# Attention with top-1 experts on one core: side slots begun 39 tiles apart, and six weight tiles of the last one made on ScalarE and VectorE

## The chip, the cores and the metric

The kernel runs on one NeuronCore of a Trainium2 chip. The core has TensorE (PE in the profile; its weight loads are PEld), VectorE (DVE), ScalarE (ACT), GpSimd (POOL) and SyncE (SP), which here only issues DMAs. Each engine runs its own instructions strictly in the order of the program. The metric is the time of one execution on the device, in microseconds, as the median of several runs.

## The reference

```python
def _attn_ref(q, k, v, tau):            # 8 batches, 8 heads, 576 rows, 64 wide
    scores = scale * np.matmul(q, k.transpose(0, 1, 3, 2))
    thresh = np.max(scores, axis=-1, keepdims=True) - tau
    scores = np.where(scores >= thresh, scores, -1000000000.0)
    scores = scores - np.max(scores, axis=-1, keepdims=True)
    attn = np.exp(scores)
    attn = attn / (np.sum(attn, axis=-1, keepdims=True) + 1e-09)
    return np.matmul(attn, v)

def _moe_ref(x, modality_id, w_gate, modality_bias, w1, w2):   # x: 4608 x 512, 8 experts
    logits = x @ w_gate + modality_bias[modality_id]
    e_idx = np.argmax(logits, axis=1)
    ...
    for e in range(E):
        mask = e_idx == e
        h = np.maximum(x[mask] @ w1[e], 0.0)          # 512 -> 1024
        out[mask] = gate_w[mask, None] * (h @ w2[e])  # 1024 -> 512
```

The attention output, with heads side by side, is the `x` of the second function.

## The kernel before

**Attention** is cut into 288 tiles of 128 query rows of one head: 9 tiles for a pair of heads (`NI`), 36 for a batch (`PB`). The main loop (line 1055) takes one tile a step: scores on TensorE (`qk_half`, tile `s`), maximum on VectorE (`nm`), exponential on ScalarE (`e`), the threshold on VectorE (`pr`), transposes of `pr` back on TensorE (`tr`), and once per pair the product with the values (`pv_half`, tile `o`, line 458). Two more steps finish what lags behind, so the loop ends at step 290.

**Routing.** When a batch's four pairs are done, `gate` and `route_a` choose the expert of each row. `route_b` counts the rows ahead of each with small matmuls on TensorE (line 458 too, `bk<-oh,ltri`), and VectorE turns the counts into a place in a table (`pos`, then `posi`). Five indirect DMAs of GpSimd (`scatter`, line 621) write row number and gate weight there. For the last batch `route_b` stands at step 300.

**Slots.** The experts' work goes in slots: one expert and up to 512 of its rows. `slot` makes three lists: events (loads of the row table `tb` and of the weights, gathers of the rows, splits of the weights), transposes of the gathered rows (`xt`, line 765), and 64 TensorE pieces for a slot of 512 rows (48 for one of 256). A piece is three matmuls (line 809 for the first layer, 835 for the second), because each float32 operand is split in a high and a low part: `hi` is a rounded copy (lines 792 or 794), `lo` the difference (796). The 1024 hidden columns are eight blocks, `f_` = 0 to 7, and the pieces come in four runs of 16: first layer of blocks 0 to 3, second layer with them, first layer of blocks 4 to 7, second layer with those. ScalarE and VectorE make `hh` and `hl` of a first-layer block (819, 820), and the second layer needs them.

**Side slots** (seven, `SIDE`) take rows of batches that are routed already, while attention goes on. `begins` says at which step each starts; its pieces are spread over the steps up to the next start (`draw`, with weights by the step's place in the pair). What is left of the queue when the loop is over follows at two pieces a step from step 290 (line 1095). **Rest slots** (`last_slot`) take all other rows. `pick_rest` chooses them after the last routing, their first transposes stand at step `F0`, and their tiles come from pools that take over the memory of attention. In them ScalarE makes every `hi`, and VectorE the `lo` of the first layer; in side slots GpSimd makes both.

**Order.** TensorE and GpSimd run in the order that these steps and events give; on ScalarE, VectorE and SyncE a scheduler decides it when the program is built. Weight tiles `raw` of side slots share four buffers, split first-layer weights three, second-layer ones five.

Of the kernel before, what the change touches and what calls it, by code (L numbers as in the profile page):

```python
# [29 lines left out]
def tile_attn_moe(  # L30
# [13 lines left out]

    C = {'prep': [0, 1, 2], 'tr0': 6, 'pv0': 7, 'tr1': 12, 'sums': 13, 'pv1': 13, 'x': 14, 'gate': [15, 16, 17, 18], 'route': 18, 'routeb': 21, 'E0': 28, 'L0': 4, 'pick': -14, 'vld': 6, 'qkld': -3, 'pre': 2.5, 'wl': 3.5, 'rows': -11, 'gat': [-9.5, -8.5, -5, -4], 'xt': [-6, -5, -2, -1], 'lc': 21, 't3': 84, 'neg': 1.0, 'draw': [2, 2, 2, 2, 1, 2, 2, 1, 2], 'last': 36, 'te': 8, 'f0': 9.5, 'sc': 1, 'warm': 24,
         'wS': [-6, -4.7, -3.4, 3, 12.5, 14, 15.5, 21.5, 4.2, 5.4, 6.6, 7.5, 22.7, 23.8, 24.9, 25.8],
# [670 lines left out]

    def slot(where, group, nrow, WT=W, wq=lambda: wp, nbuf=(4, 3, 5), lo_eng=None, xq=None):

# [65 lines left out]
        def wsplit(which, f_):  # L785
            def f():
                raw = box.pop(("raw", which, f_))
                nb = nbuf[which]
                hi = wq().tile([P, 512], F32R, name=f"w{which}h", tag=f"w{which}h", bufs=nb)
                lo = wq().tile([P, 512], F32R, name=f"w{which}l", tag=f"w{which}l", bufs=nb)  # L790
                if xq:
                    nc.scalar.copy(out=hi, in_=raw)  # L792
                else:
                    nc.gpsimd.tensor_copy(out=hi, in_=raw)
                eng = lo_eng(which, f_) if lo_eng is not None else nc.gpsimd
                eng.tensor_tensor(out=lo, in0=raw, in1=hi.bitcast(F32), op=ALU.subtract)  # L796
                box[("w", which, f_)] = (hi, lo)
            return f
# [105 lines left out]
    def at(t, f):  # L904
        events.setdefault(t, []).append(f)
# [30 lines left out]

    begins = [b * PB + C['E0'] + (C['L0'] if z == len(SIDE) - 1 else 0) for z, (_, b) in enumerate(SIDE)]
    draw = [0] * (NSTEP + 2)
# [28 lines left out]
    for n0, (w, nb) in zip(begins, SIDE):  # L967
# [4 lines left out]
        at(n0 + C['pick'], choose)  # L972
        ev, pe, xts = slot(lambda cells=cells: cells["c"], lambda: group_bank(), nb * S, w)
        at(n0 - 0.45, lambda pe=pe: work_q.extend(f for _, f in pe))
        for x, f in xts:
            put(n0 + x, f)
        times = [t for t, _ in pe]
        k0 = upto[n0]

# [159 lines left out]
```

## Time and profile before

| | |
|---|---|
| time, median of 3 runs (lowest, highest) | 1069.17 us (1068.07, 1069.84) |
| the profiled execution: its time, its span | 1063.94 us, 1062.2 us |
| PE, PEld busy | 1011.3 us (95%), 802.7 us (76%) |
| DVE, ACT, POOL busy | 715.9 (67%), 639.9 (60%), 541.2 us (51%) |
| granted TensorE clock, mean | 0.99 of full speed |

The span runs from the first to the last instruction; the profiled execution's own time is 1.7 us more. Busy time of TensorE counts matmuls that overlap, with modelled ends, so a full share does not say that it could do no more. Times inside the profile are counted from the start of the span.

### The profile page before, as it was taken

The page shows a single profiled execution, that of the slowest core. Times are in us where ns is not written, and L with a number is a line of the kernel's source. Part 1 is how long each engine was busy: PE and PEld are TensorE (multiplying, and loading weights), DVE is VectorE, ACT ScalarE, POOL GpSimd, SP SyncE. Part 2 cuts the span into 40 slices and gives each one's busy share as a digit, 9 for nine tenths or more (in the row PEclk, how much of TensorE's full clock was granted, in tenths as well). Part 3 has the DMA queues.
Part 4 walks back from the last instruction along what each step waited for, and adds up shares of the span by engine and source line. Part 5 has one row for each costly group of instructions (what it writes and reads, how often), then busy time and mean ns, then how long its engine had stood idle before and what let it go on. Part 6 is the DMA issues. An engine that isn't in the chain of part 4 may idle for free.

```text
span 1062.2 us, 20681 instructions
## 1 busy us (share of the span) xinstructions
PE 1011.3 (95%) x6652; PEld 802.7 (76%) x6652; DVE 715.9 (67%) x1773; ACT 639.9 (60%) x1474; POOL 541.2 (51%) x727
## 2 busy tenths in 40 slices
PE   7798889999999999999999999999999997999996
PEld 6576668778777787777777777788777775788885
DVE  6888888787777676876587667776677544242542
ACT  5678777676767666656666666666666522434351
POOL 2233356486738653655466643755363746443441
PEclk8999999999999999999999999999999998999999
DMA  5656677577757754566548554566555314744430
GB/s 121 147 138 148 150 179 192 144 157 202 189 138 166 189 145 130 141 192 155 146 108 221 142 144 127 149 178 155 134 122 148 122 41 131 225 133 146 146 113 25
DMA packets 212711, 156.07 MB, mean 147 GB/s; under 512 B 100846, under 2 KB 172526, under 8 KB 212592
## 3 DMA queue, kind: packets, MB, share of 16 engines
q1 hardware_dynamic: 205392, 135.72, 51.0%
q0 software_dynamic: 7200, 18.92, 5.5%
q8 instruction: 55, 0.90, 0.4%
q14 instruction: 64, 0.52, 0.2%
HBM read 84.25 MB, written 19.48 MB: 98 GB/s over the span
## 4 chain that ended last, share of the span: by engine, by line
PE 78%; DVE 9%; issue 4%; DMA 3%; POOL 2%; ACT 2%; SPq 1%; POOLq 0%; DVEq 0%; ACTq 0%
PE s L369 15%; PE bk L458 14%; PE bk L809 11%; PE bk L835 10%; PE bk L420 10%; PE pm L835 6%; PE pm L809 5%; DVE pr L404 3%; DVE nm L386 3%; PE bk L311 2%; PE bk L449 1%; PE bk L507 1%; PE bk L765 1%; DMA raw<-in_moe_w_dram 1%; PE bk L539 1%
## 5 line engine op out<-in xcount | busy, mean ns | idle before, releaser
L386 DVE TENSOR_REDUCE nm<-s 128x1 f32<-128x576 f32 x288 | 216.7, 753 | 110.5 <-PE s L369 108.7
L404 DVE SCALAR_TENSOR_TENSOR pr<-s,nm,e 128x576 f32<-128x576 f32 x288 | 231.7, 815 | 74.6 <-ACT e L392 69.1
L392 ACT ACTIVATE e<-s,nm 128x576 f32<-128x576 f32 x288 | 214.8, 746 | 95.2 <-DVE nm L386 87.1
L369 PE MATMUL s<-km,q 128*128 128x288 f32 x1024 | 199.8, 317 | 21.1 <-DVE pr L404 16.5
L431 ACT COPY ptm<-bk 128x512 f32<-128x512 f32 x256 | 149.1, 582 | 58.2 <-PE bk L420 57.6
L369 PEld LDWEIGHTS s<-km,q 128*128 128x128 f32 x1024 | 146.9, 190 | 41.8 <-DVE pr L404 25.6
L420 PE MATMUL bk<-ident,pr 128*128 128x128 f32 x1152 | 173.7, 273 | 0.3 <-ACT y L843 0.2
L420 PEld LDWEIGHTS bk<-ident,pr 128*128 128x128 f32 x1152 | 142.1, 141 | 24.0 <-DVE hl L820 0.7
L458 PE MATMUL bk<-ptm,v_m 128*64 128x320 f32 (+1 forms) x1024 | 141.4, 413 | 0.1
L796 POOL TENSOR_TENSOR w2l<-raw,w2h 128x512 fp32r<-128x512 f32 x88 | 113.5, 1297 | 33.1 <-ACT w2h L792 28.7
L284 POOL CAST nk<-str 128x64 fp32r<-128x64 f32 x31 | 7.4, 240 | 228.2 <-ACT str L298 228.2
L458 PEld LDWEIGHTS bk<-ptm,v_m 128*64 128x64 f32 x1024 | 66.5, 136 | 48.6 <-issue 7.6
L849 POOL DMA_INDIRECT out_dram<-y,tb x37 | 38.7, 1046 | 107.9 <-DVE y L847 90.4
L433 ACT COPY rp<-pr 128x64 f32<-128x64 f32 x256 | 59.0, 248 | 55.8 <-DVE pr L404 53.8
L809 PE MATMUL bk<-xh,w1h 128*128 128x512 f32 (+1 forms) x212 | 85.3, 402 | 2.0 <-ACT xh L274 1.8
L809 PE MATMUL bk<-xl,w1h 128*128 128x512 f32 (+1 forms) x212 | 76.6, 361 | 2.1 <-DVE xl L275 2.1
L809 PE MATMUL bk<-xh,w1l 128*128 128x512 f32 (+1 forms) x212 | 76.3, 360 | 0.0
L835 PE MATMUL bk<-w2h,hh 128*128 128x512 f32 x176 | 75.7, 430 | 0.0
L796 POOL TENSOR_TENSOR w1l<-raw,w1h 128x512 fp32r<-128x512 f32 x56 | 71.6, 1279 | 4.5
L796 DVE TENSOR_TENSOR w1l<-raw,w1h 128x512 fp32r<-128x512 f32 x32 | 28.1, 882 | 65.3 <-ACT w1h L792 62.8
L835 PE MATMUL bk<-w2h,hl 128*128 128x512 f32 x176 | 69.5, 395 | 0.0
L835 PE MATMUL bk<-w2l,hh 128*128 128x512 f32 x176 | 68.9, 392 | 0.0
(203 smaller groups left out, 1982.4 us busy)
## 6 DMA issues: line engine op xcount, KB each, us to landing
raw<-in_moe_w_dram SPq DMA_DIRECT2D x176, 256.0 KB, 3.4
q<-nq SPq DMA_DIRECT2D x124, 256.0 KB, 4.5
km<-nk SPq DMA_DIRECT2D x124, 144.0 KB, 2.5
v_m<-in_v_dram SPq DMA_DIRECT2D x32, 256.0 KB, 4.6
xs<-xr SPq DMA_DIRECT2D x32, 256.0 KB, 5.7
k_m<-in_k_dram SPq DMA_DIRECT2D x62, 128.0 KB, 2.7
q_m<-in_q_dram SPq DMA_DIRECT2D x62, 128.0 KB, 3.1
vr<-in_v_dram SPq DMA_DIRECT2D x64, 16.0 KB, 3.6
```

Source lines behind the costliest of these rows:

```text
L369: nc.tensor.matmul(out=sps[:, hf, 0:SH], lhsT=a, rhs=x, start=(z == 0), stop=(z == len(passes) - 1))
L386: in_line(nc.vector.tensor_reduce(out=nm[:, 0:1], in_=sv, axis=AX.XY, op=ALU.max, negate=True), two)
L392: nc.scalar.activation(out=e, in_=sv, func=AF.Exp, bias=nm[:, 0:1])
L404: in_line(nc.vector.scalar_tensor_tensor(out=pr.rearrange("p (a x) -> p a x", a=2), in0=s2[n % 2][:, :, 0:SH], scalar=nm[:, 1:2], in1=e, o ...
L420: nc.tensor.transpose(out=ps[:, kc * P:(kc + 1) * P], in_=pr[:, kc * P:(kc + 1) * P], identity=ident)
L431: nc.scalar.copy(out=ptm[:, s, :, (c % 2) * P:(c % 2 + 1) * P], in_=pv)
L433: nc.scalar.copy(out=rp[:, i, :], in_=pr[:, SA:S])
L458: nc.tensor.matmul(out=o, lhsT=lhsT, rhs=rhs, start=start, stop=stop, skip_group_check=True)
L796: eng.tensor_tensor(out=lo, in0=raw, in1=hi.bitcast(F32), op=ALU.subtract)
L809: nc.tensor.matmul(out=ps[:, 0:WT], lhsT=a[:, cs], rhs=x[:, c, :], start=(c == 0 and z == 0), stop=(c == KC - 1 and z == 2))
L835: nc.tensor.matmul(out=ps, lhsT=h[:, ts], rhs=w, start=(z == 0 and y == 0), stop=(z == F2 - 1 and y == 2))
L849: i = _inst(nc.gpsimd.indirect_dma_start(out=out, out_offset=bass.IndirectOffsetOnAxis(ap=tb[:, t, 0:1].bitcast(U32), axis=0), in_=y, in_o ...
```

## The change

The last six side slots took turns of 36 tiles, except that the last began 4 tiles later. Now each slot of 512 rows begins 39 tiles after the one before it. The seven starts were steps 64, 100, 136, 172, 208, 244 and 284, and are 64, 100, 136, 175, 214, 253 and 292. Of the 416 pieces, 363 stood inside the loop and 53 behind it; now it is 348 and 68, so the last side slot lies wholly behind the loop. `F0` moves from step 311 to step 316, while the last batch's routing stays at step 300: between its matmuls and the first transposes of the rest slots stand 32 pieces where there were 22. In the last side slot the weights of blocks 5, 6 and 7 of both layers get their high part from ScalarE and their low part from VectorE.

```diff
-    C = {'prep': [0, 1, 2], 'tr0': 6, 'pv0': 7, 'tr1': 12, 'sums': 13, 'pv1': 13, 'x': 14, 'gate': [15, 16, 17, 18], 'route': 18, 'routeb': 21, 'E0': 28, 'L0': 4, 'pick': -14, 'vld': 6, 'qkld': -3, 'pre': 2.5, 'wl': 3.5, 'rows': -11, 'gat': [-9.5, -8.5, -5, -4], 'xt': [-6, -5, -2, -1], 'lc': 21, 't3': 84, 'neg': 1.0, 'draw': [2, 2, 2, 2, 1, 2, 2, 1, 2], 'last': 36, 'te': 8, 'f0': 9.5, 'sc': 1, 'warm': 24,
+    C = {'prep': [0, 1, 2], 'tr0': 6, 'pv0': 7, 'tr1': 12, 'sums': 13, 'pv1': 13, 'x': 14, 'gate': [15, 16, 17, 18], 'route': 18, 'routeb': 21, 'E0': 28, 'lag': 3, 'late': ((1, 5), (1, 6), (1, 7), (2, 5), (2, 6), (2, 7)), 'pick': -14, 'vld': 6, 'qkld': -3, 'pre': 2.5, 'wl': 3.5, 'rows': -11, 'gat': [-9.5, -8.5, -5, -4], 'xt': [-6, -5, -2, -1], 'lc': 21, 't3': 84, 'neg': 1.0, 'draw': [2, 2, 2, 2, 1, 2, 2, 1, 2], 'last': 36, 'te': 8, 'f0': 14.5, 'sc': 1, 'warm': 24,
...
-    def slot(where, group, nrow, WT=W, wq=lambda: wp, nbuf=(4, 3, 5), lo_eng=None, xq=None):
+    def slot(where, group, nrow, WT=W, wq=lambda: wp, nbuf=(4, 3, 5), lo_eng=None, xq=None, late=()):
...
-                if xq:
+                if xq or (which, f_) in late:
                     nc.scalar.copy(out=hi, in_=raw)
                 else:
                     nc.gpsimd.tensor_copy(out=hi, in_=raw)
-                eng = lo_eng(which, f_) if lo_eng is not None else nc.gpsimd
+                eng = lo_eng(which, f_) if lo_eng is not None else nc.vector if (which, f_) in late else nc.gpsimd
                 eng.tensor_tensor(out=lo, in0=raw, in1=hi.bitcast(F32), op=ALU.subtract)
...
-    begins = [b * PB + C['E0'] + (C['L0'] if z == len(SIDE) - 1 else 0) for z, (_, b) in enumerate(SIDE)]
+    begins = [b * PB + C['E0'] + C['lag'] * max(0, z - 2) for z, (_, b) in enumerate(SIDE)]
...
-        ev, pe, xts = slot(lambda cells=cells: cells["c"], lambda: group_bank(), nb * S, w)
-        at(n0 - 0.45, lambda pe=pe: work_q.extend(f for _, f in pe))
+        ev, pe, xts = slot(lambda cells=cells: cells["c"], lambda: group_bank(), nb * S, w,
+                           late=C['late'] if n0 == begins[-1] else ())
+        at(min(n0 - 0.45, NSTEP + 1), lambda pe=pe: work_q.extend(f for _, f in pe))
...
-        k0 = upto[n0]
+        k0 = sum(FC * KC + FC * (x // P) for x, _ in SIDE[:begins.index(n0)])
```

The order of the instructions moves with it at three places that matter below. The first is VectorE just behind the routing matmuls of the last batch. Before, the ranks went straight on to the table places:

```order
L602 TENSOR_TENSOR pos_11486<-bk0_162,base_144 128x48
L604 COPY base_144<-pos_11486 128x8
L605 TENSOR_TENSOR pos_11486<-pos_11486,creg_119 128x40
L657 SCALAR_TENSOR_TENSOR left_11550<-done_145,base_144 1x8
L607 TENSOR_TENSOR pos_11486<-pos_11486,oh_11444 128x40
```

The same place of the changed kernel:

```order
L602 TENSOR_TENSOR pos_11409<-bk3_165,base_144 128x48
L796 TENSOR_TENSOR w1l_11639<-raw_11569,w1h_11638 128x512
L820 SCALAR_TENSOR_TENSOR hl_11399<-bk1_163,hh_11398 128x512
L604 COPY base_144<-pos_11409 128x8
L605 TENSOR_TENSOR pos_11409<-pos_11409,creg_119 128x40
L657 SCALAR_TENSOR_TENSOR left_11465<-done_145,base_144 1x8
L607 TENSOR_TENSOR pos_11409<-pos_11409,oh_11371 128x40
```

The low part of the last side slot's first-layer weights of block 6 and the `hl` of its block 3 now stand inside the chain. The second place is SyncE behind the table load of the first rest slot (`tb`). Before, that slot's own first-layer weights followed it:

```order
L739 DMA tb_11650<-tab_140 128x4x2
L775 ISA
L775 DMA raw_11727<-in_moe_w1_dram 128x4x128
L775 ISA
L775 DMA raw_11747<-in_moe_w1_dram 128x4x128
```

In the changed kernel:

```order
L739 DMA tb_11619<-tab_140 128x4x2
L779 ISA
L779 DMA raw_11633<-in_moe_w2_dram 128x512
L775 ISA
L775 DMA raw_11710<-in_moe_w1_dram 128x4x128
L775 ISA
L775 DMA raw_11729<-in_moe_w1_dram 128x4x128
```

`raw_11633` is the side slot's second-layer weight of block 7; it moved behind the table load. The third place is ScalarE in the same stretch. Before, the `hh` of blocks 4, 5 and 6 of the side slot (`hh_11618`, `hh_11673`, `hh_11702`) came first, and one cast of a rest slot's weight stood ahead of block 7's (`hh_11719`):

```order
L819 ACTIVATE hh_11618<-bk3_165 128x512
L819 ACTIVATE hh_11673<-pm_11626 128x512
L819 ACTIVATE hh_11702<-pm_11681 128x512
L792 CAST w1h_11777<-raw_11727 128x512
L819 ACTIVATE hh_11719<-pm_11706 128x512
L792 CAST w1h_11815<-raw_11747 128x512
```

In the changed kernel, where `w2h_11689` and `w1h_11671` are the side slot's block 7 and `hh_11652` and `hh_11685` its blocks 4 and 5:

```order
L792 CAST w2h_11689<-raw_11633 128x512
L792 CAST w1h_11755<-raw_11710 128x512
L792 CAST w1h_11793<-raw_11729 128x512
L792 CAST w1h_11671<-raw_11592 128x512
L819 ACTIVATE hh_11652<-pm_11629 128x512
L792 CAST w1h_11843<-raw_11767 128x512
L792 CAST w2h_11872<-raw_11782 128x512
L792 CAST w1h_11890<-raw_11819 128x512
L792 CAST w2h_11979<-raw_11835 128x512
L819 ACTIVATE hh_11685<-pm_11664 128x512
L792 CAST w2h_11989<-raw_11862 128x512
L792 CAST w2h_12004<-raw_11882 128x512
```

Every cast but `w1h_11671` takes a weight that SyncE loads behind the table. The `hh` of blocks 6 and 7 follow only behind the last of these rows.

## Rows read from the trace of the kernel before

**Rows 1.** Windows: us, busy us (instructions) of PE, PEld, DVE, ACT, POOL, clock, DMA share, GB/s

```profile
500.00:820.00 320.00, 318.39 (x2121) 250.74 (x2120) 230.93 (x602) 204.99 (x478) 170.69 (x227) 1.00 0.58 146
...
868.40:902.80 34.40, 28.07 (x113) 21.22 (x113) 19.06 (x59) 9.76 (x17) 24.05 (x23) 0.85 0.34 102
...
881.40:884.80 3.40, 3.23 (x8) 2.61 (x9) 0.00 (x0) 0.00 (x0) 0.12 (x1) 0.55 0.00 0
884.80:891.30 6.50, 4.19 (x17) 2.80 (x16) 2.05 (x4) 2.24 (x4) 3.29 (x4) 1.00 0.70 197
891.30:898.20 6.90, 5.78 (x19) 4.30 (x18) 2.48 (x4) 2.94 (x6) 5.26 (x4) 0.51 0.92 309
```

**Rows 2.** Chain that ended last, inside the loop: start us, us, what

```profile
601.32 2.84 PE bk L458 x20
...
629.04 2.84 PE bk L458 x20
...
659.19 2.84 PE bk L458 x20
...
717.04 2.84 PE bk L458 x20
...
721.74 0.70 PE bk L809 x3
...
743.40 2.84 PE bk L458 x20
...
772.93 2.84 PE bk L458 x20
```

**Rows 3.** Timeline of PE behind the loop: start, us, what [idle before <-releaser]

```profile
868.48 0.20 PE L458 MATMUL bk<-oh,ltri 128*128 128x48 bf16 x1
...
880.21 0.50 PE L809 MATMUL pm<-xh,w1h 128*128 128x512 f32 x1 [2.27 <-POOL w1h L794]
...
881.57 0.80 PE L809 MATMUL pm<-xh,w1l 128*128 128x512 f32 x1 [0.63 <-POOL w1l L796]
...
889.76 0.50 PE L835 MATMUL pm<-w2h,hh 128*128 128x512 f32 x1 [2.20 <-ACT hh L819]
...
893.23 1.09 PE L765 MATMUL bk<-ident,xg 128*128 128x128 f32 x4 [1.12 <-DMA xg<-xs,tb]
...
899.19 0.60 PE L765 MATMUL bk<-ident,xg 128*128 128x128 f32 x4
...
902.85 0.40 PE L809 MATMUL pm<-xh,w1h 128*128 128x512 f32 x1
...
919.60 0.50 PE L835 MATMUL pm<-w2h,hh 128*128 128x512 f32 x1 [1.40 <-ACT hh L819]
```

**Rows 4.** Timeline of DVE: the ranks, the table places, a low part of a weight

```profile
868.82 0.21 DVE L602 TENSOR_TENSOR pos<-bk,base 128x48 f32<-128x48 f32 x1 [1.38 <-PE bk L458]
...
873.00 0.15 DVE L612 CAST posi<-posf 128x5 int32<-128x5 f32 x1
...
895.37 0.69 DVE L796 TENSOR_TENSOR w1l<-raw,w1h 128x512 fp32r<-128x512 f32 x1 [2.97 <-ACT w1h L792]
```

**Rows 5.** Timeline of POOL: the last of the five table scatters

```profile
878.57 0.97 POOL L621 DMA_INDIRECT tab<-pay,posi  x1 [0.30 <-issue]
```

**Rows 6.** Timeline of SP: table load of the first rest slot, then weights

```profile
884.33 0.38 SPq L739 DMA_DIRECT2D tb<-tab  x1
885.38 1.87 SPq L775 DMA_DIRECT2D raw<-in_moe_w_dram  x3
```

**Rows 7.** Waits of SP from 860 to 900 us: in total, times, longest

```profile
SPq L739 <- DMA tab<-pay,posi: 3.0, 1, 3.0
```

**Rows 8.** Timeline of ACT: first and eighth cast of that slot's weights, an hh between

```profile
888.60 0.62 ACT L792 CAST w1h<-raw 128x512 fp32r<-128x512 f32 x1 [9.96 <-DMA raw<-in_moe_w_dram]
889.12 0.59 ACT L819 ACTIVATE hh<-pm 128x512 fp32r<-128x512 f32 x1
...
898.02 0.62 ACT L792 CAST w2h<-raw 128x512 fp32r<-128x512 f32 x1 [1.16 <-DMA raw<-in_moe_w_dram]
```

## Prediction

> **What bounds the kernel now.** I read the windows first. From 500 to 820 us TensorE is busy for 318.39 of 320.00 us at full clock, and every other engine for less than three quarters of that [rows 1]. The reader is to see that the loop is bound by TensorE, so a piece of side-slot work that leaves the loop takes its TensorE time with it. The last batch's routing matmuls start at 868.48 (R below), and the first piece of a rest slot at 902.85 [rows 3]; in the 34.40 us between, TensorE is busy for 28.07 at a mean clock of 0.85 [rows 1]. The timeline of TensorE shows why. It stops for 2.27 and 0.63 us for block 7's first-layer weight of the last side slot, which GpSimd makes behind the scatters; for 2.20 us for the `hh` that follows; for 1.12 us for gathered rows; and later, at 919.60, for 1.40 us for an `hh` of a rest slot [rows 3]. Sum: 7.6 us. In two stretches the clock is at its lower level of 1.2 GHz: 0.55 over 3.23 busy us and 0.51 over 5.78 [rows 1], which costs 3.23 x 0.45 + 5.78 x 0.49 = 4.3 us. Ahead of the first such stretch stands the stop of 2.27, ahead of the second the one of 2.20. So some 12 us behind R are open to be won or lost.
>
> **Term 1: fewer pieces ahead of R.** 15 pieces leave the loop. Their price is read from the chain, where the same matmuls of line 458 return once a pair: 27.72 us from 601.32 to 629.04 with 16 pieces between by the program's order, 26.36 from 717.04 to 743.40 with 14; 30.15 from 629.04 to 659.19 with 16, 29.53 from 743.40 to 772.93 with 15 [rows 2]. Three pieces fewer take 1.36 + 0.62 = 1.98 us off, 0.66 each. The three matmuls of a piece stand there with 0.70 [rows 2], the upper bound; a loop that in part waits for other engines would give less, and I bound it by 0.50, well below what the two comparisons give (0.68 and 0.62). I take 0.66: 15 x 0.66 = -9.9 us (-7.5 to -10.5).
>
> **Term 2: from R to the first piece of a rest slot.** This is a chain from VectorE to the weights. Before: `pos` starts at R + 0.34, `posi` ends at 873.15 = R + 4.67 [rows 4], the last scatter starts 5.42 later [rows 5], the table load is issued 5.76 behind that [rows 6], after a wait of 3.0 for the scatters [rows 7], and the first weight load 1.05 later [rows 6]. The eighth cast of those weights starts 12.64 behind that issue, the first 3.22 [rows 6, 8].
>
> Now the low part of block 6's weight (0.69 [rows 4]) and an `hl` (a like operation, taken as 0.69) stand ahead of the copy of `base` on VectorE. The low part needs ScalarE's cast (0.62 [rows 8]), and that cast needs the buffer that block 3's last first-layer matmul frees, about at R. The copy follows at R + 0.62 + 0.69 + 0.69 = R + 2.0 instead of R + 0.55: +1.5 us (1.2 to 1.6). So `posi` ends at R + 6.2, the last scatter starts at R + 11.6, the table is loaded at R + 17.4 and the first weight load goes at R + 18.4.
>
> That first load is now the side slot's second-layer weight of block 7, and eight of the rest slot follow. SyncE issues in order, so it can't go before the table. On ScalarE the `hh` of blocks 5, 6 and 7 stand among or behind the casts of these nine, so TensorE, once it has done what it can, waits for loads. Two waits follow.
>
> First, block 7's first layer. TensorE reaches it 28 pieces behind R at 0.70 each, R + 20.0. Its cast stands behind three casts of new loads, the first of which can start at R + 18.4 + 3.2 = R + 21.6; four casts and a low part later the weight is there, at R + 24.1 or a little after. A stop of 4.1 us takes the place of 2.27 + 0.63 + 2.20 = 5.1.
>
> Second, and later, so that it decides: the last load. Nine loads land 12.64 + 0.85 behind the first issue (the ninth, 256 KB, at the 309 GB/s of the busiest stretch [rows 1]), at R + 31.9. A cast (0.62), two `hh` (0.59 each [rows 8]) and the `hl` (0.69) end at R + 34.4. Then TensorE does the rest of a piece, two sets of transposes (0.60 each [rows 3]) and four pieces, 4.2 us: R + 38.6. TensorE stops on the way for longer than the 2.20 that preceded the second low-clock stretch, so I add one stretch of half clock like the first (3.23 x 0.45 = 1.4): R + 40.0. Against 34.4 that is +5.6 us (+4.2 without the clock; to +8 with the slower loads below).
>
> Here a page speaks for less. The first stretch of loads runs at 197 GB/s and a DMA share of 0.70, the second at 309 and 0.92 [rows 1]. The Trainium skill, "DMA: Bandwidth & Descriptors", section "Where 436 GB/s comes from", says that a transfer from HBM to SBUF is bound by the HBM side at some 358 GB/s; by that figure nine loads and four gathers of 262 KB, 3.4 MB, would take 9.5 us instead of 13.5, and the sum would be 4 us lower (an estimate). No stretch here reaches it.
>
> **Term 3: pieces that stand later.** The last side slot has 8 pieces left when the rest slots begin where it had 3 (56 of 64 done, before 61). Five at 0.70: +3.5 us. The other ten of the fifteen lie inside term 2, under its waits.
>
> **Term 4: the stop at 919.60.** The `hh` that TensorE waits for there stands behind casts whose loads came late [rows 3]; by the new order no cast of a late load stands ahead of it: -1.4 us (0 to -1.5).
>
> **Costs that are hidden.** Six casts (0.62) and six subtractions (0.69) go to ScalarE and VectorE; GpSimd's took 5.26 / 4 = 1.3 us each in the last stretch [rows 1]. In the loop VectorE and ScalarE are busy for 230.93 and 204.99 of 320 us, so there is room; behind R their places cost what term 2 says. In turns of 39 tiles, the split of block 7 in a normal side slot waits for a buffer for up to 0.9 tile (about 2.8 us) on GpSimd, with gathers behind it; GpSimd is busy for 170.69 of 320 us [rows 1], and the rows are gathered tiles ahead. If that cover failed, TensorE would stop for up to 2.8 us in each of four slots. The last slot's last gather, near the end of the loop, has the same cover less some 1 us. The rows that each pick takes are the same, so no slot changes its size.
>
> **Sum.** -9.9 + 5.6 + 3.5 - 1.4 = -2.2 us against the profiled execution's 1063.94, 1061.7 there. The median of the runs is 1069.17, 5.2 above that execution; taken off the median, the forecast is 1067.0.
>
> **Rivals.** *The loads are slower* (it ends slower than before). Gathers and nine loads, 13 x 262 KB = 3.4 MB, run throughout at the 197 GB/s of the stretch at 884.80 [rows 1]: they take 17.3 us instead of 13.5, +3.8, and TensorE stands long enough for a second half-clock stretch like the one at 891.30, of which some 1.7 us are not waited out anyway. Sum +3.3: 1072.5. It decides when the first rest piece lies past R + 42.2 (no gain) or R + 44.4 (slower by 2.1). For it speaks that the last `hh` are queued behind nine casts; against it that the first half of the old loads ran at that rate and the second at 309.
>
> *The loads come as they are issued* (a larger gain). The first three issues take 1.87 us [rows 6], 0.62 each, and the first lands after 3.2. If all nine keep that, the last is there at R + 18.4 + 8 x 0.62 + 3.2 = R + 26.6, the casts of ScalarE are hidden by block 7's pieces, and the first rest piece comes at about R + 35: sum -7.2, 1062.0. Against it stand the old loads, of which the eighth needed 12.64. The skill's 358 GB/s ("DMA: Bandwidth & Descriptors", same section) would lie near this case, at about -6.
>
> *The loop gives back less.* If waits on ScalarE and VectorE take the place of the pieces, 0.50 each, 15 give -7.5 and the sum is +0.2: 1069.4, no change. For it: side-slot pieces are the filler between the attention's steps. Against it: both comparisons of [rows 2].
>
> **How the numbers follow.** The forecast as worked out has 0.50, its own range is 1065.0 to 1069.2 (term 2 from 4.2 to 7.0, term 1 by 0.8 either way); the larger gain 0.18, the smaller loop gain 0.15, the slow loads 0.17. A measurement of this kernel can tell about 0.2%, 2.1 us, from no change; the runs before spread over 1.8. The forecast lies at that edge: of its 0.50 some 0.26 fall beyond it, 0.23 within, 0.01 slower. Larger gain: 0.17 faster, 0.01 same. Loop: 0.01 faster, 0.12 same, 0.02 slower. Slow loads: 0.01 same, 0.16 slower. Sums: faster 0.44, same 0.37, slower 0.19. The range from 1062.5 to 1071.0 cuts off the outer parts of the first and the last rival, about 0.1 on either side.
>
> **What would show it.** Term 1: the marks of line 458 come closer by 0.66 us for each piece fewer, R lies near 858.6. Term 2: `posi` ends at R + 6.2 with a low part and an `hl` ahead of the copy, the table is issued at R + 17.4, TensorE stops about 4 us ahead of block 7's first layer for a cast, then again for an `hh` behind casts that wait for loads, and the first rest piece stands near R + 40 with a stretch at about half clock before it. Term 4: no stop of over 1 us in the first rest slot for an `hh`. The prediction is wrong if R moves by less than 7.5 us, if the table is issued before R + 16, or if the last of the nine casts starts before R + 28 or past R + 36.

## The result, and the profile after

The changed kernel took 1054.70 us (median of 4 runs, 1053.85 to 1055.24) beside 1068.62 for the kernel before (1066.30 to 1069.84): ratio 0.9882, 95% interval 0.9865 to 0.9900. That is 13.9 us faster, below the range of 1062.5 to 1071.0. Its profiled execution took 1054.34 us, that of before 1063.94: 9.6 us between the two traces. The other 4.3 us are runs of before that took longer than its profiled one, and no trace shows them.

In the later sets of runs the gain was smaller. Three controls of the changed kernel (after_again, after_third, after_fourth), on the chips that the record numbers 12, 3 and 1 (for the first set it names none), gave 0.9962 (0.9948 to 0.9977), 0.9955 (0.9938 to 0.9973) and 0.9942 (0.9922 to 0.9962), 5 to 8 us. Each is a ratio to the kernel before in the same set. The experiments below are read against these controls.

The windows of the changed kernel (us, then busy us and instructions of PE, PEld, DVE, ACT and POOL, clock, DMA share, GB/s), which answer to [rows 1]:

```profile
500.00:820.00 320.00, 317.57 (x2124) 248.74 (x2123) 231.74 (x602) 207.36 (x483) 176.27 (x229) 1.00 0.61 149
856.60:891.80 35.20, 32.65 (x144) 25.37 (x143) 19.77 (x65) 15.13 (x26) 18.18 (x17) 0.95 0.42 121
...
879.60:883.10 3.50, 3.50 (x9) 2.74 (x10) 2.17 (x3) 1.99 (x5) 1.49 (x3) 0.51 1.04 385
```

The loop is as full as it was. Behind the routing matmuls TensorE is busy for 32.65 us where it was busy for 28.07, in nearly the same time. The timeline of TensorE there, which answers to [rows 3]:

```profile
856.67 0.20 PE L458 MATMUL bk<-oh,ltri 128*128 128x48 bf16 x1
...
878.76 0.50 PE L809 MATMUL pm<-xh,w1h 128*128 128x512 f32 x1 [2.14 <-ACT w1h L792]
...
886.32 0.50 PE L835 MATMUL pm<-w2h,hh 128*128 128x512 f32 x1 [0.34 <-ACT hh L819]
...
891.74 0.40 PE L809 MATMUL pm<-xh,w1h 128*128 128x512 f32 x1
```

R moved from 868.48 to 856.67, by 11.8 us. The first rest piece stands at R + 35.1, where it stood at R + 34.4. The stops between are 2.14 and 0.34 us in place of 2.27, 0.63, 2.20 and 1.12. The chain on VectorE, which answers to [rows 4]:

```profile
857.02 0.21 DVE L602 TENSOR_TENSOR pos<-bk,base 128x48 f32<-128x48 f32 x1 [0.24 <-PE bk L458]
857.33 0.69 DVE L796 TENSOR_TENSOR w1l<-raw,w1h 128x512 fp32r<-128x512 f32 x1
857.94 0.68 DVE L820 SCALAR_TENSOR_TENSOR hl<-bk,hh 128x512 fp32r<-128x512 f32 x1
858.54 0.16 DVE L604 COPY base<-pos 128x8 f32<-128x8 f32 x1
...
859.20 0.36 DVE L662 SCALAR_TENSOR_TENSOR th<-th_lo,left 1x72 f32<-1x72 f32 x2
...
859.50 0.15 DVE L612 CAST posi<-posf 128x5 int32<-128x5 f32 x1
```

The low part and the `hl` stand ahead of the copy as forecast, which comes at R + 1.87. But `posi` ends at R + 2.98, not R + 6.2. The same stretch of the kernel before, first VectorE, then GpSimd, shows what was missed:

```profile
870.59 2.48 DVE L662 SCALAR_TENSOR_TENSOR th<-th_lo,left 1x72 f32<-1x72 f32 x2
```

```profile
870.45 2.54 POOL L796 TENSOR_TENSOR w2l<-raw,w2h 128x512 fp32r<-128x512 f32 x2
```

Two small operations (`th`), 0.18 us each in the changed kernel, took 1.24 each while GpSimd subtracted, and ended with its second subtraction. In the changed kernel GpSimd splits nothing there. The rest of the chain (GpSimd's last scatter; SyncE; ScalarE's first and last cast of the nine loads and the two `hh` behind), which answers to [rows 5 to 8]:

```profile
865.08 0.97 POOL L621 DMA_INDIRECT tab<-pay,posi  x1 [0.30 <-issue]
```

```profile
871.62 0.37 SPq L739 DMA_DIRECT2D tb<-tab  x1
872.26 0.35 SPq L779 DMA_DIRECT2D raw<-in_moe_w_dram  x1
```

```profile
875.01 0.62 ACT L792 CAST w2h<-raw 128x512 fp32r<-128x512 f32 x1 [6.03 <-DMA raw<-in_moe_w_dram]
...
885.15 0.62 ACT L792 CAST w2h<-raw 128x512 fp32r<-128x512 f32 x1 [0.45 <-DMA raw<-in_moe_w_dram]
885.67 1.08 ACT L819 ACTIVATE hh<-pm 128x512 fp32r<-128x512 f32 x2
```

The table load goes at R + 14.95 (forecast 17.4), the first weight load at R + 15.6 (18.4), the last cast starts at R + 28.5 (31.9) and the last `hh` ends at R + 30.1 (33.7).

### The profile page after: what moved, and what is told of

Read it like the earlier page. It is cut to its first block, busy times and chain, and to the rows that moved or that the text cites. A ratio compares the mean times of both kernels' runs of the same rounds, so it can differ in the third digit from the quotient of the medians.

```text
span 1052.4 us, 20681 instructions
## 1 busy us (share of the span) xinstructions
PE 1008.2 (96%) x6652; PEld 802.1 (76%) x6652; DVE 715.2 (68%) x1779; ACT 643.5 (61%) x1480; POOL 531.0 (50%) x715
## 5 line engine op out<-in xcount | busy, mean ns | idle before, releaser
L369 PE MATMUL s<-km,q 128*128 128x288 f32 x1024 | 199.5, 317 | 20.5 <-DVE pr L404 15.4
L796 POOL TENSOR_TENSOR w2l<-raw,w2h 128x512 fp32r<-128x512 f32 x85 | 111.2, 1315 | 31.2 <-ACT w2h L792 27.0
L809 PE MATMUL bk<-xh,w1h 128*128 128x512 f32 (+1 forms) x208 | 82.8, 398 | 0.9 <-ACT xh L274 0.9
L835 PE MATMUL bk<-w2h,hh 128*128 128x512 f32 x164 | 70.9, 432 | 0.0
L796 POOL TENSOR_TENSOR w1l<-raw,w1h 128x512 fp32r<-128x512 f32 x53 | 68.0, 1283 | 4.3
L796 DVE TENSOR_TENSOR w1l<-raw,w1h 128x512 fp32r<-128x512 f32 x35 | 31.1, 891 | 52.2 <-ACT w1h L792 52.1
L835 PE MATMUL bk<-w2h,hl 128*128 128x512 f32 x164 | 64.6, 394 | 0.0
L835 PE MATMUL bk<-w2l,hh 128*128 128x512 f32 x164 | 64.3, 392 | 0.0
```

The costliest lines, as they stand in the source:

```text
L369: nc.tensor.matmul(out=sps[:, hf, 0:SH], lhsT=a, rhs=x, start=(z == 0), stop=(z == len(passes) - 1))
L809: nc.tensor.matmul(out=ps[:, 0:WT], lhsT=a[:, cs], rhs=x[:, c, :], start=(c == 0 and z == 0), stop=(c == KC - 1 and z == 2))
L835: nc.tensor.matmul(out=ps, lhsT=h[:, ts], rhs=w, start=(z == 0 and y == 0), stop=(z == F2 - 1 and y == 2))
```

## The experiments

"Span behind R" is the span less R, taken from the first line of `ltri` in each trace. Each ratio is that to the kernel before in the same set of runs.

| run | median us (before beside it) | ratio, 95% interval | R | first rest piece | span behind R |
|---|---|---|---|---|---|
| before, two traces | | | 868.5; 877.6 | R + 34.4; 35.1 | 193.7; 194.2 |
| changed, first | 1054.70 (1068.62) | 0.9882, 0.9865 to 0.9900 | 856.7 | R + 35.1 | 195.7 |
| after_again | 1067.86 (1073.10) | 0.9962, 0.9948 to 0.9977 | 871.8 | R + 34.6 | 195.1 |
| after_third | 1068.12 (1072.98) | 0.9955, 0.9938 to 0.9973 | 870.3 | R + 34.7 | 194.9 |
| after_fourth | 1067.13 (1075.44) | 0.9942, 0.9922 to 0.9962 | 870.0 | R + 35.2 | 195.7 |
| lag_only | 1073.98 (1074.04) | 1.0008, 0.9989 to 1.0026 | 870.4 | R + 41.1 | 201.4 |
| late_only | 1073.20 (1074.04) | 0.9991, 0.9970 to 1.0012 | 878.5 | R + 33.0 | 195.3 |
| late_f0 | 1072.14 (1073.10) | 0.9994, 0.9979 to 1.0008 | 876.4 | R + 36.0 | 194.1 |
| last_only | 1073.11 (1074.04) | 0.9996, 0.9979 to 1.0013 | 876.5 | R + 36.3 | 196.4 |
| lag2 | 1081.76 (1072.98) | 1.0087, 1.0056 to 1.0118 | 887.0 | R + 34.1 | 192.2 |
| pool_busy | 1068.75 (1074.04) | 0.9956, 0.9937 to 0.9975 | 870.1 | R + 36.1 | 196.4 |
| sc3 | 1068.71 (1075.44) | 0.9944, 0.9927 to 0.9961 | 869.0 | R + 35.2 | 195.4 |
| f0_12 | 1069.54 (1072.98) | 0.9962, 0.9940 to 0.9984 | 870.1 | R + 32.6 | 196.3 |
| w17_first | 1071.35 (1073.10) | 0.9983, 0.9962 to 1.0005 | 870.5 | R + 38.1 | 198.7 |
| act_manual | 1067.20 (1072.98) | 0.9941, 0.9922 to 0.9961 | 870.4 | R + 35.0 | 195.6 |
| act_f0_17 | 1064.04 (1075.44) | 0.9911, 0.9885 to 0.9938 | 869.3 | R + 33.7 | 193.3 |
| act_f0_17b | 1067.82 (1076.00) | 0.9938, 0.9919 to 0.9958 | 870.8 | R + 35.0 | 193.4 |
| act_f0_19 | 1068.82 (1075.44) | 0.9955, 0.9934 to 0.9977 | 870.6 | R + 35.6 | 196.0 |
| dve_lo | 1070.26 (1076.00) | 0.9946, 0.9928 to 0.9965 | 873.1 | R + 34.2 | 192.9 |

### The parts of the change, one by one

The starts alone:

```diff
-'late': ((1, 5), (1, 6), (1, 7), (2, 5), (2, 6), (2, 7))
+'late': ()
```

> The changed kernel with the six late weight tiles back on GpSimd; the starts stay 39 tiles apart. Theory 1: part of the gain comes from the chain behind the routing matmuls (at R), because GpSimd no longer splits weights there, which held the scatters and stretched VectorE's small operations (0.63 and 1.24 us each before, 0.18 after). Then posi ends at R + 4.5 or later instead of R + 2.98, the table load goes 1.5 us or more later than R + 14.95, and the time is 1056.5 to 1060. Theory 2: the pieces that leave the loop carry the whole gain. Then the time stays within 2 us of 1054.7.

The gain is gone, but not by the chain: `posi` ended at R + 3.4. The timeline of TensorE:

```profile
896.54 0.80 PE L809 MATMUL pm<-xh,w1h 128*128 128x512 f32 x1 [6.12 <-POOL w1h L794]
...
905.69 0.51 PE L835 MATMUL pm<-w2h,hl 128*128 128x512 f32 x1 [1.55 <-DVE hl L820]
```

GpSimd splits the weight of block 7 behind the rest slot's gathers, and TensorE waits 6.12 us for it. All that the starts gave in the loop is lost there. The text ahead says that GpSimd and TensorE follow the steps as written; by the code that holds inside the loop, and behind it the scheduler orders them too, which is how this split came to stand so late.

The late tiles alone, with the old starts. In late_only the first transposes stand at step 311 again (`f0` 9.5), in late_f0 at 316:

```diff
+    begins = [b * PB + C['E0'] + (4 if z == len(SIDE) - 1 else 0) for z, (_, b) in enumerate(SIDE)]
```

> The kernel before with its old starts, but the six late weight tiles on ScalarE and VectorE. Theory 1 (the chain): posi ends at R + 3.5 or earlier instead of R + 4.67, the stop of 2.27 us for GpSimd's split behind the scatters goes, R stays near 868.5, and the time falls by 3 to 5.5 us from before. Theory 2 (only the pieces count): within 2 us of before.

> The kernel before with its old starts, with the six late weight tiles on ScalarE and VectorE and with the rest slots' first transposes at step 316, as in the changed kernel; only the starts of the side slots are the old ones. With the late tiles alone TensorE stopped for 7.46 us at the first transposes, for gathered rows. Theory 1 (fill): the chain from the routing to the gathered rows takes some 23 us whatever TensorE does, and the change gains behind the routing by having 32 pieces in that time where there were 22. Then this stop falls under 1.5 us, the time is 5 to 8 us under that of the late tiles alone, 4 to 9 us under before. Theory 2 (starts): without pieces taken from the loop nothing is gained; then it is within 2 us of before.

Neither can be told from the kernel before. `posi` ends at R + 2.6 and GpSimd's stop is gone in both, yet TensorE gets no further. First late_only, then late_f0:

```profile
901.70 1.09 PE L765 MATMUL bk<-ident,xg 128*128 128x128 f32 x4 [7.46 <-DMA xg<-xs,tb]
```

```profile
901.78 0.66 PE L765 MATMUL bk<-ident,xg 128*128 128x128 f32 x4 [1.48 <-DMA xg<-xs,tb]
902.77 1.35 PE L765 MATMUL bk<-ident,xg 128*128 128x128 f32 x8 [0.33 <-DMA xg<-xs,tb]
...
912.15 0.45 PE L765 MATMUL bk<-ident,xg 128*128 128x128 f32 x1 [8.03 <-DMA xg<-xs,tb]
```

In late_only the stops moved to the gathered rows, which the first transposes find at R + 23.2 (901.70 - 878.49). In late_f0, with one side piece left behind them, the next slot's transposes come at once, and its gathers were issued only from 908.77 on. Removing a wait without work to put in its place moves it.

Only the last slot moved, the others as before:

```diff
+    begins = [b * PB + C['E0'] + (12 if z == len(SIDE) - 1 else 0) for z, (_, b) in enumerate(SIDE)]
```

> The changed kernel, but the third to sixth slot keep their old starts and only the last one starts at step 292, so that as many pieces stand behind the loop as in the changed kernel; the sixth slot's 64 pieces are spread over 48 tiles instead of 39, and slots three to five keep 16 pieces a pair. Theory 1: the number of pieces that leave the loop decides, at 0.7 to 0.8 us each, wherever they leave it. Then R is 856.7 within 1 us and the time within 2 us of 1054.7. Theory 2: the even spacing is worth something by itself, since the filler of a denser slot waits for its weights. Then R is 859 or more and the time 1057 or more.

R came at 876.5, 4.7 us behind the control's, with one piece more in the loop (349). The eight pieces fewer in the last batch of the loop saved nothing: TensorE stopped there for `q`, whose loads are queued on SyncE behind a table load that waited 18.1 us for scatters, and the clock was at its lower level for 3.41 us. The scatters were late because GpSimd, with the split of a weight ahead of them, had waited 17.68 us for that weight's buffer, which TensorE's pieces still used.

```profile
797.78 0.61 POOL L794 CAST w1h<-raw 128x512 fp32r<-128x512 f32 x1 [17.68 <-PE bk L809]
```

```profile
823.00 1.27 PE L369 MATMUL s<-km,q 128*128 128x288 f32 x4 [2.77 <-DMA q<-nq]
...
827.39 0.77 PE L369 MATMUL s<-km,q 128*128 128x288 f32 x4 [0.99 <-DMA q<-nq]
```

Starts 38 tiles apart, with the first transposes two steps earlier, at step 314:

```diff
-'lag': 3, ... 'f0': 14.5
+'lag': 2, ... 'f0': 12.5
```

> The changed kernel with starts 38 tiles apart and the first transposes at step 314: 356 pieces in the loop, 8 more than in the changed kernel, 7 fewer than before. Theory 1 (term 1): each piece in the loop costs about 0.7 us and the same 0.7 us behind it, so that only what fills stops is gained; by the second chip's loop, 5.8 us for 15 pieces, R comes 3 us later than in the changed kernel, and the time is 1 to 4 us above it. Theory 2: the gain is a matter of where slots meet the batches' own loads and writes; then R moves by less than 1 us or by more than 5.

The second theory, and far: R lies 16.8 us behind the control's (887.0 to 870.3) for 8 pieces more, and the kernel is slower than before. Of TensorE's stops 16 us stand between the fourth and the eighth routing where the control has 9. The windows from the first routing to the last (columns as above), first after_third, then lag2, divide the difference:

```profile
125.20:870.20 745.00, 724.23 (x4955) 568.25 (x4955) 537.95 (x1400) 477.65 (x1128) 412.82 (x545) 1.00 0.61 153
```

```profile
124.40:887.00 762.60, 733.03 (x4979) 573.22 (x4979) 539.84 (x1402) 480.26 (x1131) 412.49 (x545) 0.99 0.60 150
```

The 24 matmuls of 8 pieces are there. Of the 17.6 us more, 8.8 are busy time, of which 1.7 come from 3.41 us more at half clock; that leaves 0.9 a piece. The other 8.8 are stops (the window less its busy time), 29.6 us beside 20.8. So a piece's own work has a fairly steady price; the stops and the half clock that come on top do not, and in this run they are over half of the loss. Where the slots' loads and splits meet those of the batches has moved in all six slots; which meeting makes which stop was not followed.

### The loop's price in the later sets

> The changed kernel unaltered, as a control beside the kernel before on the same chip: the first four runs stood on a chip where the kernel before took 1074.0 us, 5.4 more than where the change was first measured. Theory 1: the change keeps its gain whatever the level of the chip; then it is faster than before by 11 to 15 us here too. Theory 2: the gain of 13.9 us held a part that belongs to those executions (profile against profile the change gained 9.6 us); then it is faster by 4 to 9 us.

> The kernel before unaltered, for a second profile. The profiled execution of before took 1063.94 us where its other runs took 1066.3 to 1069.8. Theory 1: the difference lies behind the routing matmuls, where stops let the clock fall for a longer or shorter stretch; then R is at 868.5 within 1 us and the rest is longer. Theory 2: it lies in the loop; then R is later by most of the difference.

> The changed kernel unaltered, the control for the three other runs of this set, and once more against before: 9 to 14 us faster if this chip is like the first one, 4 to 7 us if it is like the second.

> The changed kernel unaltered, the control of this set: by the two chips measured after the first, 4 to 7 us faster than before; by the first, 11 to 15.

The span behind R differs by 0.5 us between the two traces of before; R differs by 9.1. So the level lies in the loop. There the change moved R by 11.8 us in the first pair of traces and by 5.8 in the second (877.6 to 871.8). The routing matmuls, first and last of eight, in before_again and after_again:

```profile
L458 PE MATMUL bk<-oh,ltri x8: 186/196/199, 124.7 to 877.6; 128*128 128x48 bf16 x8
```

```profile
L458 PE MATMUL bk<-oh,ltri x8: 186/197/197, 124.8 to 871.8; 128*128 128x48 bf16 x8
```

The windows between these two, in before, changed, before_again and after_again:

```profile
124.20:868.40 744.20, 730.38 (x5000) 575.12 (x5000) 539.23 (x1400) 479.56 (x1131) 418.14 (x551) 1.00 0.61 154
```

```profile
124.30:856.60 732.30, 718.74 (x4955) 566.71 (x4955) 537.80 (x1400) 478.10 (x1128) 413.56 (x545) 1.00 0.63 156
```

```profile
124.70:877.60 752.90, 735.71 (x5000) 576.62 (x5000) 538.26 (x1400) 479.46 (x1131) 418.14 (x551) 1.00 0.60 152
```

```profile
124.80:871.80 747.00, 726.48 (x4955) 569.00 (x4955) 537.38 (x1400) 477.66 (x1128) 412.85 (x545) 0.99 0.61 153
```

The 45 matmuls of the 15 pieces are gone in both pairs, and TensorE's busy time falls by 11.6 us in the first (0.78 a piece) and by 9.2 in the second (0.62; 0.73 without what 3.41 us more at half clock cost). What differs is the rest: TensorE's stops are 13.8 and 13.6 us in the first pair, 17.2 and 20.5 in the second. The pieces gave their time back in both; in the second, 3.3 us went to more stops and 1.7 to the half clock.

One place where the later sets are slower is this operation of ScalarE, first in before, then in before_again:

```profile
320.37 0.58 ACT L431 COPY ptm<-bk 128x512 f32<-128x512 f32 x1 [0.47 <-PE bk L420]
```

```profile
327.02 0.58 ACT L431 COPY ptm<-bk 128x512 f32<-128x512 f32 x1 [3.75 <-PE s L369]
```

ScalarE stands for 3.75 us, although the matmuls named had ended earlier, and VectorE for 2.03 beside it. TensorE stops 1.33 us behind them, and 6.83 us at half clock follow. Such stops come some 9 to 14 us behind a batch's routing, in every trace of the later sets. GpSimd issues its scatters there, and these were moved:

```diff
-'sc': 1,
+'sc': 3,
```

> The changed kernel with every batch's table scatters on GpSimd two tiles later. On the second and third chip TensorE stops in the loop some 8 to 13 us behind each batch's routing matmuls (1.8, 1.1 and 2.3 us in one profile), when VectorE and ScalarE stand still with their visible waits over, while GpSimd issues the five scatters of the batch; on the first chip the same program does not stop there. Theory 1: the scatters hold the others up; then these stops move by two tiles (about 6 us) or vanish. Theory 2: the stops belong to the output rows that are written at this place (x of the pair), and stay 8 to 13 us behind the routing matmuls.

In after_fourth, the control on the same chip, TensorE stops for 1.80 us near 552, 2.30 near 669 and 1.81 near 785; with the edit 1.21, 0.62 and 0.60 are left there, and the time didn't change. But the edit is no clean test. The scatters hardly moved where the first of these stops stayed: the first of the five stands 4.5 us behind the fifth routing in both, and in the other batches 0.8 to 3.6 us later than in the control. And a new stop of 3.50 us, with 3.41 us at half clock behind it, stands behind the second routing:

```profile
222.65 1.22 DVE L641 SCALAR_TENSOR_TENSOR done<-pk_a,done 1x8 f32<-1x8 f32 x1
```

```profile
226.23 0.48 PE L449 MATMUL bk<-ident,rp 128*128 128x128 f32 x1 [3.50 <-ACT ptm L431]
```

There GpSimd's splits came ahead of the moved scatters, and two small operations of VectorE took 1.27 and 1.22 us where the control has 0.22 and 0.14. So this run neither shows the scatters to be the cause nor clears them. In the first traces the same scatters stand at the same places without such stops, so they are not enough by themselves. The waits themselves are for TensorE's results: in after_third VectorE waits 3.28 us for transposes that the trace shows ended at 546.44.

```profile
549.95 0.69 DVE L510 TENSOR_TENSOR xr<-bk,ri 128x512 f32<-128x512 f32 x1 [3.28 <-PE bk L522]
```

Why VectorE and ScalarE go on so late stays open.

### Behind the routing: chain, order or fill

GpSimd kept busy inside the chain:

```diff
+            for _ in range(5):
+                nc.gpsimd.tensor_tensor(out=dum, in0=dum, in1=base[:, 0:1].to_broadcast([P, 128]), op=ALU.subtract)
```

> The changed kernel with five idle subtractions of 128x128 on GpSimd added behind the copy of base, at R + 1.9, some 1.7 us in all, ahead of the scatters. They compute nothing that is used. Theory 1 (contention): while GpSimd subtracts, VectorE's small operations of the chain take 0.4 to 1.2 us instead of 0.15 to 0.36, and posi ends at R + 4 or later instead of R + 2.98. Theory 2 (the queue alone): VectorE's operations keep their lengths, posi ends at R + 3.0, and only the first scatter waits, for GpSimd's own work. Either way the time rises by 0.5 to 2 us.

Single operations of the chain took up to 0.40 us, `posi` ended at R + 3.5, and the table load went at R + 15.6 where after_again has 14.0, in part because the five subtractions stand ahead of the scatters with 2.4 us. The effect on the chain is there and small, since these subtractions are short. The median is that of the controls, by its ratio; in the trace the first rest piece comes at R + 36.1 beside 34.6 to 35.2, and the span behind R is 0.7 to 1.5 us longer.

Four pieces fewer between the routing and the transposes:

```diff
-'f0': 14.5
+'f0': 12.5
```

> The changed kernel with the rest slots' first transposes at step 314 instead of 316, so that 28 pieces instead of 32 stand between the routing matmuls and them. Theory 1 (fill): those ten added pieces, and not a shorter chain, took the place of the stops, so four fewer bring back 1.5 to 3 us of stops in front of the transposes (gathered rows) or of the last hh, and the time rises by 1 to 3 us. Theory 2: the last loads set the first rest piece and the pieces only change places; then within 1 us of the changed kernel.

The stop at the transposes came back, and a stretch of 3.41 us at half clock with it:

```profile
893.18 0.63 PE L765 MATMUL bk<-ident,xg 128*128 128x128 f32 x4 [3.17 <-DMA xg<-xs,tb]
```

The span behind R grew by 0.6 to 1.4 us over the controls; the medians don't tell the two apart.

GpSimd's order written out, with block 7's first-layer weight split ahead of the gathers:

```diff
-'late': ((1, 5), (1, 6), (1, 7), (2, 5), (2, 6), (2, 7))
+'late': ((1, 5), (1, 6), (2, 5), (2, 6), (2, 7))
...
-            ev.append((t - 8, gather(t)) if xq else (None, gather(t), C['gat'][t - TT]))
+            ev.append((t - 5, gather(t)) if xq else (None, gather(t), C['gat'][t - TT]))
...
+        at(304 if b == B - 1 else step[0] + C['sc'], lambda: scatter(b, posi))
...
+    with tc.manual_schedule(engines={ET.Pool}):
+        run_events(0, F0 - 3)
     run_events(0, 10 ** 9)
```

> The changed kernel with GpSimd's order behind the loop written out: the first-layer weight of block 7 is split by GpSimd again, but ahead of the gathers of the first rest slot, block 4's stands behind the scatters, and these gathers go 3 steps later. Theory 1: the stop of 2.14 us ahead of block 7's first layer, which waited for ScalarE's cast behind three casts of new loads, goes, and with it the half clock behind it (3.41 us at half speed); then it is 2 to 4 us faster than the changed kernel. Theory 2: the loads behind the table are the limit, and TensorE waits as long in front of the last hh; then within 1 us of it.

Slower than the control by 3.5 us. With block 4's split behind the scatters, its buffer came free late, and so did the load of block 7's weight. GpSimd waited 6.90 us for that load with the gathers queued behind it, and the transposes stopped TensorE for 4.54 us.

ScalarE's order written out, with the first transposes where they were (act_manual), then with `f0` at 17.0 (act_f0_17, and again on another chip) and at 19.0 (act_f0_19):

```diff
+    with tc.manual_schedule(engines={ET.Activation}):
+        run_events(0, F0 + 8)
     run_events(0, 10 ** 9)
```

> The changed kernel with ScalarE's order behind the loop written out in the order of TensorE's work, up to step 324: the cast of block 7's first-layer weight and every hh of the last side slot stand ahead of the casts of the rest slot's weights. Theory 1 (the prediction's second term): what TensorE loses behind the routing matmuls it loses to ScalarE's order, an hh or a cast behind casts that wait for loads. Then the stops of 2.1 to 2.5 and 0.3 to 1.1 us go, the first rest piece stands at R + 32 to 33 instead of 34.6 to 35.1, and the time falls by 2 to 4 us from the changed kernel. Theory 2: the chain routing, table, gathers, loads sets the time. Then the stops come back at the first transposes or at the rest slot's first weights, and the time stays within 1 us.

> ScalarE's order written out as in the run before, and the rest slots' first transposes 2.5 steps later, so that 37 pieces instead of 32 stand between the routing matmuls and them. Theory 1 (fill): TensorE needs about R + 26 us of work until the gathered rows are there, whatever the order of the others; five pieces more (3.5 us) remove the stop of 3.32 us at the transposes and the half clock behind it, and the time falls by 3 to 4.5 us from the same kernel without them (1067.2 there). Theory 2: the wait moves on to the rest slot's first weights; then within 1.5 us of it.

> The run with ScalarE's order and 37 pieces once more, as the control of the next one: 9 to 12 us faster than before.

> The same with 41 pieces between. Theory 1 (fill): once the stop is gone further pieces only change places; within 1 us of the run with 37. Theory 2: something else of the rest slots, late weights or their rows, needs those pieces behind the transposes; then 1 us or more slower than with 37.

With ScalarE in order (act_manual) the stops for its cast and its `hh` are gone, and one of the same size stands at the gathered rows; the time is that of the control within 1 us. First act_manual, then act_f0_17, then act_f0_19:

```profile
896.49 0.63 PE L765 MATMUL bk<-ident,xg 128*128 128x128 f32 x4 [3.32 <-DMA xg<-xs,tb]
```

```profile
915.14 0.50 PE L809 MATMUL pm<-xh,w1l 128*128 128x512 f32 x1 [1.12 <-DVE w1l L796]
```

```profile
923.09 0.50 PE L835 MATMUL pm<-w2h,hh 128*128 128x512 f32 x1 [3.08 <-ACT hh L819]
```

Five pieces more removed the stop at the gathered rows in act_f0_17 and left 1.39 us of it in act_f0_17b; the span behind R fell to 1.5 to 2.4 us below the three controls in both. In medians that was 3.1 us less than the control on one chip (1064.04 to 1067.13); on the next chip, without a control, the ratio was 0.9938, no better than the best control. With nine pieces more an `hh` of the rest slot is late instead, and the median on the chip of act_f0_17 is 4.8 us higher than its (1068.82 to 1064.04). So order alone gave nothing that could be measured, order with five pieces more a gain that shows behind R in two traces and in one median of two, and nine pieces more gave none over the control (0.9955 beside 0.9942).

The subtractions off GpSimd:

```diff
-lambda which, f_: nc.vector if which == 1 else nc.gpsimd
+lambda which, f_: nc.vector
```

> The same with the low parts of all second-layer weights of the rest slots on VectorE instead of GpSimd. Theory 1 (contention): in the control a low part of a first-layer weight, 0.69 us elsewhere, took VectorE 5.28 us while GpSimd made four subtractions of 5.04 us in all, and TensorE stopped 1.12 us for it; with no subtraction left on GpSimd there no low part takes over 0.8 us, that stop goes, and the time falls by 1 to 2 us, although VectorE has more to do. Theory 2 (order alone): the long operation is a wait of its own, for the cast or a buffer, and VectorE with more to do is later still; then a stop of about 1 us stays there and the time is the same or more.

The stop went, and no low part takes longer than 0.74 us. In act_f0_17b, on the same chip, VectorE and then GpSimd:

```profile
912.49 5.28 DVE L796 TENSOR_TENSOR w1l<-raw,w1h 128x512 fp32r<-128x512 f32 x1 [0.34 <-ACT w1h L792]
```

```profile
912.16 5.05 POOL L796 TENSOR_TENSOR w2l<-raw,w2h 128x512 fp32r<-128x512 f32 x4
```

The same low part without them:

```profile
914.17 0.68 DVE L796 TENSOR_TENSOR w1l<-raw,w1h 128x512 fp32r<-128x512 f32 x1
```

It is GpSimd's subtraction that holds VectorE. The whole gains nothing: the span behind R is 0.5 us shorter than in act_f0_17b, an `hh` stops TensorE for 0.84 us a little later, and the ratios overlap. The median is even 2.4 us higher (1070.26 to 1067.82); in the traces R comes 2.3 us later, though the edit leaves the loop as it was.

## Why the prediction was wrong

**Term 2** (+5.6 us from R to the first rest piece) is the step that failed. The traces gave +0.7 in the first pair and -0.5 in the second. Three things in it were off.

First, the chain. "+1.5 us" counted what was put on VectorE and not what was taken off GpSimd. The two operations stand where they were forecast and the copy comes at R + 1.87 (forecast 2.0); but from the copy's start to the end of `posi` it took 1.1 us in place of 4.1, because GpSimd's subtractions no longer held the small operations. `posi` was 3.2 us earlier than forecast, and the last cast 3.4. The sign that the prediction had set, a table load before R + 16, came true. A rule on this stands in the Trainium skill, "SBUF — State Buffer", section "Who interferes with whom": a VectorE instruction with two inputs in SBUF contends with a GpSimd instruction that reads there, over a port pair that the page calls an exclusive lock. These traces agree (1.24 us for 0.18, 5.28 for 0.69) and go further: 5.28 us is four GpSimd instructions, not one. The row of 2.48 us lay in the trace of before and was not asked why it was long.

Second, the half clock was added where it is hidden. 1.4 us were added to the time at which the wait for the last `hh` ends. The stretch came (3.50 us at 0.51), but ahead of that `hh`, for which TensorE would have waited anyway: the stop there was only 0.34 us. (The working also puts the weight of block 7 at R + 24.1, which has the four casts but not the low part; that wait enters no sum, and TensorE went on there at R + 22.1.)

Third, the loads, a small part: the last cast stood 12.9 us behind the first issue instead of 13.5. On average they were no faster than before, 266 GB/s from the first issue to the last cast beside 265; the 385 GB/s above are the peak of 3.50 us. In that stretch the transfers went faster than the 358 GB/s quoted in the prediction from the Trainium skill, "DMA: Bandwidth & Descriptors", section "Where 436 GB/s comes from"; over the whole run of loads they stayed below it.

What the traces put in its place is fill under an earlier chain. Behind R stand 10 pieces more before the first rest piece, 7.0 us. The stops there fell from 6.2 to 2.5 us, and what the half clock costs from 4.3 to 3.50 x 0.49 = 1.7: 7.0 - 3.7 - 2.6 = +0.7, as measured. The prediction did place these pieces "under its waits", but let the waits grow by as much. The runs do not divide the two cleanly: late_only has the early chain with the transposes at their old place, and TensorE stops for 7.46 us at the gathered rows. Act_manual and f0_12 bear the fill out from the other side: the rows are there some 23 to 26 us behind R, and with 28 to 32 pieces of 0.70 us TensorE stops for what is missing.

**Term 1** (-9.9) was -11.8 in the first pair and -5.8 in the second; its bounds of -7.5 and -10.5 were too tight on either side. The price itself was not far off: TensorE's busy time fell by 0.78 and 0.62 a piece (0.73 without the half clock) where 0.66 was taken. What the term put at nothing is what a shift of six slots against the batches does to TensorE's stops and clock: nothing in the first pair, 3.3 and 1.7 us in the second. The stretches from which 0.66 was read differ by one or two pieces in an otherwise like place and could not show it. Lag2 and last_only show it more strongly.

**Terms 3 and 4** (+3.5 and -1.4, together +2.1) gave +1.3 and +1.4 from the first rest piece to the end. The stop at 919.60 went, as forecast; only the size is off, by under a microsecond.

**The sum** for the profiled executions was -2.2 and is -9.8 in span: 1.9 from term 1, 4.9 from term 2, 0.8 from terms 3 and 4. **The scale**: to set the forecast off the median assumed that before and changed kernel lie equally far from their profiled executions. They don't: before 4.7 us, the changed kernel 0.4.

Of the rivals the one with early loads came nearest in number: first rest piece at R + 35, as it has it. That is luck. It needs the last load 8.2 us behind the first issue, and the last cast stood 12.9 behind it; R + 35 came by the earlier chain. The rival of a small loop gain (-7.5, waits in place of the pieces) is near what the second pair shows, -5.8 with 3.3 us more of stops; the slow loads appear in no trace.

## What to carry to other kernels

Where a chain of small steps ends a phase, moving work under it can be worth as much as the chain's stops, and no part of such a change need gain anything alone: here parts of the change (starts with later transposes, late tiles, late tiles with later transposes) gave ratios of 0.9991 to 1.0008, and the whole 0.9942 to 0.9962 in the later sets. Read how long each small operation of the chain takes beside its twins elsewhere: those that were several times longer here were held by another engine, and the edit that took work off that engine shortened the chain. And a price per piece from a periodic loop holds for the piece's own work; what the shift does to the stops around it comes on top and can eat half of it, so read TensorE's stops as well as its busy time, in a second set of runs too.

## What was not expected of the hardware

A VectorE subtraction of 0.69 us took 5.28 while GpSimd made four of its own in 5.05 us, and ended only behind the last of them. The same programs ran 9 (before) and 15 us (changed) longer in the loop in the traces of the later sets, in part as stops of 1 to 2.3 us that the first traces don't have. Whether the chip or something else differs between the sets was not tested, and why ScalarE and VectorE stand there is not settled.
